# A block-sparse attention and gated feed-forward kernel: PSUM tiles of the last output blocks, a crossbar transpose for the second segment, and a new written-out order

## The chip, the core and the metric

The kernel runs on one core of a Trainium2 chip. A core has engines that run side by side, each taking its own instructions strictly in order: TensorE (PE, matrix products, with its weight loads shown apart as PEld), VectorE (DVE), ScalarE (ACT), GpSimd (POOL) and SyncE (SP), which issues DMAs. Products land in PSUM, and DVE or ACT copy them to SBUF. The metric is the device time of one execution in microseconds, the median of several runs. Lower is better.

## The reference

Inputs are q, k, v of shape 4 x 8 x 768 x 64 (batch, heads, tokens, head width), three sampled key blocks for each of the 24 blocks of 32 tokens, and the weights of a feed-forward part. The result has shape 4 x 768 x 512.

```python
scores = scale * np.matmul(q, k.transpose(0, 1, 3, 2))
# kept: neighbouring blocks, first and last block (as query or key), the sampled ones
scores = np.where(mask, scores, -1000000000.0)
attn = np.exp(scores - max); attn = attn / sum
x = np.matmul(attn, v)                  # then heads side by side: 4 x 768 x 512
h = np.maximum(x @ w_in, 0.0)           # 512 -> 1024
conv_out[s] = conv_w[0] * h[s-1] + conv_w[1] * h[s] + conv_w[2] * h[s+1]
gate = 1.0 / (1.0 + np.exp(-conv_out))
out = (h * gate) @ w_out                # 1024 -> 512
```

## The kernel before

**Segments and units.** The 4 x 768 query rows are cut into nine segments (`SEGS`): seven of 384 rows, numbered 0 to 6, then segment 7 with 256 rows and segment 8 with the last 128. The attention is cut into 144 units. A unit is eight score blocks of 128 x 128: up to eight score products into one of two PSUM tiles `st` (L761, 1024 columns in all), one exponential of 128x1024 on ACT (L773) into one of six tiles `pt`, and eight products with V, 65 columns each (L798; the 65th column is the row sum). The mask rides along as 24 extra rows of the score product. A segment of 384 rows has 18 units, four head pairs (hp) of 4.5 units each.

**After a head pair.** DVE takes the reciprocal of the sums (L707) and the normalised product (L709) into `xtok`. Then `xtok` is turned so that features lie on partitions (`xT`). Segments in `X_PE` do it on PE (L728, three products of 128 columns for a head pair of 384 rows, into a PSUM tile `mix`) and copy the result out with DVE or ACT; all others do it with one crossbar DMA that SP issues (L718).

**Feed-forward of a segment.** Eight first products (f1, L895) of four matmuls each go into one of two PSUM tiles `mix`; ReLU on ACT (L915) or DVE (L917) writes `hE`; the convolution is six multiplies (L947) and two adds (L955) on DVE for each pair of feature chunks (in segment 8 it is done on PE, L966); the sigmoid is a tanh on ACT (L994, L971), then L997 and L1002 on DVE write `gT`. A row block of 128 rows (t = 0 to 5 in a batch) is finished by the second products (f2, L830): four steps a = 0 to 3 of two matmuls with 512 columns each, step a needing the gates of chunk pair a. Then a copy to SBUF (L327 on ACT or L331 on DVE) and an output DMA on SP (L839).

**The last blocks.** `out_block` is called with `tail` for the two blocks that end with segment 8, t = 4 and t = 5 of the last batch. Before, they accumulate in halves of the two `st` tiles, which hold scores until then: block 4 in the left half of `st0`, block 5 in two pieces of 256 columns in the right half of `st0` and the left half of `st1`. Blocks 2 and 3 use the two `mix` tiles. Blocks 2, 3 and 4 need segment 7's gates; block 5 needs only segment 8's.

**The order.** No scheduler runs when the kernel is built. All operations are listed in a graph, and the string `ORDER` (found beforehand by a search over a model of the program; two characters name an operation, one its engine where it has a choice, one each buffer it takes) says in which order they are put down, and so in which order each engine runs them. `put_down` (L95) reads it. Costs and due times in the graph serve only that search.

**The start.** PE begins with `NWARM` + `NFILL` dummy products (L230): 13 of 256 and 26 of 128 columns, the latter strewn among the first real ones. Head pair 0 is loaded in fp32 over SP and ACT's queue, cast, turned on PE and copied to the slot tiles `t`; the mask rows are built on DVE meanwhile.

**Loads.** From head pair 6 on, q and k are also turned by crossbar DMAs of SP (L597, tiles `stg`), then copied by DVE (L331). SP runs them in the order of the string, together with L718 and the output DMAs.

Of the kernel before, what the change touches and what calls it, by code (L numbers as in the profile page):

```python
# [20 lines left out]
0G0002119030405060F18011a0708090a0b0c0d0e0H0f0g0h0i0I0J0M0N0R0O0Q0P0ZA1uV00S0T1wA0YA1xA1y01E11zV01FA0WV0VA0U0j
0k0l1B00m0n0o0p1N11O1I01Z01/21AA202b1171CV1DV11G1vA0XV520535715810V5401G012V1HV1b0q0r0s0t0u0v0w0x0y5c00z5911P1
0A5d0K1S02d32e1V12725h11MA0135e25i5501QV11UV1TV1RV565a5b1J05m05n5j32r04M2p2140B5f0C5v15w5o45g5k5x51LV1KV1+V10L
1e11f5A05B2102415C05F15G0D0E5K05L5l5p5H15M25q15y22V225V26V23V5T15U5V35r02cV25z5D5s155Y05Z5E2f15+4611625I5J2i0
6352gV3660676802hV2kV2jV5N5O5W06b16c5X1W15/6d16k06l60646p16m26q65695P15Q6r3161i1XV2qV36a6e6g26h1h6u06v6f16n6o
6z16A6s6t6w46i06I06J1YV1j1k1d5t16x6y6B56N16C6O5uV06jV6K06D6P15R16S06T6U26L06M6E26F5SV6G00+6HV6X16Q1o6Y2s4N2l34O
2D04P1p1m2F14Q1c1n2G4R1q4S2EV42R16Z31lih1ii70071ie0ifigV0ijA7917a724ik1il2807e07f7b5iC0iEiD29V2aViFimA7g06R7j1
7k7l1in16VioipV6W7o07p2t06+iG7x17y6/iw173ix7q27z34T1r4U2T24ViK1iL2uV47502vViM767C07DiyA7417c7d7H17E47I2w17h7i
2m02xV2oV2yV7m7M07n7r7s7A07B7J52nV7N7t1iN77178V12SV07F7R17Siq0iriH7O07T17uiIisViJ0iO7+07/7G7K7L831848028537v1
2H07P7wV2IV07Q8807UiP7W22JViQ7V1898d181827X8a42U4W1s8e86it1iuivV4X1t4Y2+2iR8f58m08n7Y0878b7ZV8r18s8o08c2K18g8t1  # L30
iS2iT2MV8w08x8hiz08y28B18C8i02LV8jiAiBViV8p0iU8G08H8q8u8v8k18D3i+3j0iWi/8I48O18P8Q5j608T08U8V0322iX8z8A8E8F8J
8Y18K18R8S8Z2W02V12X8lV2ZVj12YV8+1910j792932j2jc1jd9919a8W8X8/90j39e09f944Z3034+31iYiZ2/V1959b3j8je9g59j19kj4
8L1j50/331349628M8N2jfjgV09l136V39j9jaA19o09p9q4jl13a03c9t1jmji0jnA35V9u971gjjjkV9B03e04/370509Cjr1js9c09d9v0
2z0512N1jG0jHjI3b3i9G19H2A09hjJ2CV2BVjK9D29L09i9MjtA9I39m9N5jo1jpjqV9Q1jx09Rjy9n9r9sjLjzA9S19Y09wju1jvjwA9Z3l
3m13o38V29x19EjO1jMjPjQjR9y0jW29+4a119F9Ja2jX9zjA0a60a7a30a823j13n3u3x3y2jSjT9K9O9P2O12PVjN2QVjZjYab19Tac9U9/0
jBjCV9V1983fjU9Wag0j+jb3q13d33p4ad3jD1aha0ai5jEjFAao1apa4a59Ak23ks0a9k3jV9Xk4k5k6aq1j/aaaeafat0auajak1ay1arav4
kg1asazkhaA0aD0awktaEaxk7aL1aMaBaCk0k1aF2kiku3raN3aQ0aRk8k9aGkjaS1aHkvkkA2al2am3hV3AaV1aWa+0a/3v2kwA3aX5b00aI0
aJ3gV3sV3C0ky1kz3kV3kAV1kB0kCkDVkW0kXkZaO0b31aPb4b52kN1aTbb0kH0aU3z3G3H03J3K33M3L3R3S1kIkOkJAkPAbcbg1bhbd4kY3tV
k+kE0kFkGVl21l3l4l5l6aYaZb1b2b6bl0kK1b71bebmbi3bfbq1kLbrkMVb81an0km0knbjla2lck/bn1by0lb3wV43B0ldbzl0b9kokpbs5l7
bA0kqA1bD1kT1bEkUbI0bJkQ0bF2kVAbK4l8leaKkxkl3N1kRkSVli3lkl11lfbN1l9ljlgllbkbobpbtbubv2lmka1bObP3bS0bT3Dlhbw3EV  # L40
3FVbU1kbkckdbB0keA3b+1b/c05bCbGbHlw0bLc30c4lxc81lnbMbQc9lq1lrc50ba3Ololpbxcd0ce3U3V03Z3Wkf3XjhlybRlzbVbW1ca2cf4
3PV13QVlAV2c1cl1cmcq0c2lscrcn3lC0lDcv13IV03TV1bX0bYcwcs1ltcx5lEVlF0lGlBlHVl+0l/m0m1m2cA0cBc6c7cblI0cF1cccGluA3
cC046471lJcgchlL1co0cH2lMcN0cpctcOlKAlNVci1m61m7cjcucS1cTm3cylO0lR1cP3cU13+0bZ1cX0cYczlPcDcElScZ5lQAm8m9cIcJ1m4
mamb3Y43lTVme2mgmfcK2mccLmhm5d01d1d80cQcRcVcWc+d9lU0lVd24da0dd1lWVdec/lX1df24b4849ck4c13/di0djd3lYdn1domdmidk3
d4cMdb04k4l2lZAdcmA0ds0dtmu14424adgdp1mm3momnmpd50mqdhd6du4mjmkml4pdA1dBmBdld7dC0mr40V242msdF0dGdmdqmvdrdvdw1
dK1dLdDdEdH2mCmwdIdP0dQdM3dR1mtmDmEV0lvdX1dYdx1dymxdJdNdOdSe00dTdZ44m4h4dmyA24ykre1e51e20e6e75mS0mV1mWd+0mTdz2
41VdU2dVea0ebef1mUV0mXAne0nfngnhni4q0dW4z3d/ege34n4i04D4Am/1e4ec3mY0en0eon0n1V4oeh1e8es1ete9edmZ4eV3m+V4fVnm1nn
45V2ep4njnknpnoeeeiek0elnqnl0mF4E1mzex0eymG1mHmImJez0eu5n20eC0mKA3eDej1eqereK1n3eE3em4rn4AeLeM4nrevn51n6eP0eweA
n7VeQeBeFeGeN0nb0eU1eVnu2eH1eInweR5eW0n81ncn9naAeZ0e+f21eOf3e/3nvnxmM1mNeSeTeXeYfa0f44ndVnsny4jV3nznC3fbf0f1nt
f5ff1f61fgfc5fh0mOeJmPnDnEfdfk0o00flnFfefp1o1mQA1o31fqo4nGnH4sV4nAnB4tVo2Afm3nInJo5AnQ0nR4B4v4w14CmRmL4Ffx0fy  # L50
4xV4oq0osfr2nSnK1fz4fC1fDnTfH04J4K2fIfE14LV0orotounUV0fJ5ovnLnMnNfM1fNnOA2f724GV0f84HVfifR0fjnW0nXnZ1n+fnfO0nYA
n/AfS4ufofsftfZ1f+o90owoxfA0oaoi1okfT3ojfu0olfvomg20fBg3fFo61o7f/2g44obAg71fGfKfLg8fPfQo8Voy2fUozfW1onnVf904g4I
fwof0gc0g91oBoooAopgdge5oc1odoeAgk1ogohAglfV1g0g1g5gp0gm0oU1gqg6gaoVgu1gbgvgfggoO0oPoCoG3oHoJoIfXoKgr3oDgw2gn0
gD0gogsgtgEgI1gJoLgh2oEoFgigF4fYgK1oWgxoQgN0gOoMoNoXoYV1gP5gygW1oRgXp41p5p6g/0p7gjoSA3h0gY0gz0p8A0pa0pbpd1peh41
pcV1pfVpy0gAh13pAh5hd0pj0pg1pkphgG1h62nPoZplApiAhegHgLhi1gMgQgRhf4pzpBgB0gCA1gZ0g+hjpp1pG1pCpHpIpJpKhn0hk1pDpq
pm0pnpoAprAgS1gThohw1pO2pPpEpRhxhy5h2h3h7h8ps0pto+1o/hg1p0hhpuAp1h92pQpLhp0pMpF1pShahB1gU0hChlhmhqhrp2A2gVAhs0
hthD3pv1pwhb0hz0hK0pxAhcVpThLhM2pNhu0hvVhAhT1hUqh1hEqipW3pYqn0hY0hG1qoqjApXpZp+hV4hF1hNhOq21p/hZi51i6qpApUhHpV
q0hP2q3hW0hI0q4q1h+1q5hJV2hXqe0qfhQqy0qAqzi70qBh/i01i8i9q6A1qk1qgAi10i2i30qlqO1qq2ia1qrqPibi4AqmAp9p3qtqsqG3q80
q9hR1hSAqaic1idAqbqcA0rf1rgrhAr60r7quqvqCqIqRqwq7qdoTqxr8AqDrx0rc1rdryreAri1rjr90raqEqFrz2rk0r01rAqHrBqJrlrmqK
qQrs0rtr1rbArn1ru2qW0rorp0rqrrqLqXrC0rI1rO2rJrPrvqSrwqMqTqUqNrDrQrKrRrLrMA2rSArNqVr2rTr3r4V1r5qYqZq+A0q/rErF  # L60
# [53 lines left out]
def kernel(  # L114
# [701 lines left out]
    def out_block(b, t, due, deps, after, tail=False, last=False):  # L816
# [1 line left out]
        halves = ((0, 256), (256, 512)) if last else ((0, 512),)  # L818
        outs = []
        for x, (c0, c1) in enumerate(halves):  # L820
            mb = Buf(P_tail if tail else P_mix)
# [4 lines left out]
            prev = None
            for a in range(4):
                def fn(e, a=a, acc=acc, c0=c0, c1=c1):
                    for ffc in (2 * a, 2 * a + 1):
                        nc.tensor.matmul(out=acc(), lhsT=gT_t[gb.index][:, ffc, 128 * t:128 * t + 128],  # L830
                                         rhs=woutb[:, ffc, c0:c1], start=(ffc == 0), stop=(ffc == NFFC - 1),
                                         skip_group_check=True)
# [41 lines left out]
    relu = {}  # L874
    for n, (b, g, tok, C, _) in enumerate(SEGS):
        lastn = n == NSEG - 1
        base = T(ustart[n + 1]) + 4
# [6 lines left out]
        for fg in range(NFFC // FB):  # L884
# [18 lines left out]
            def rl(e, fg=fg, hb=hb, heb=heb, tok=tok, C=C, FB=FB, w1=w1):  # L903
# [12 lines left out]
                else:  # L916
                    nc.vector.tensor_scalar(out=dst, in0=src, scalar1=0.5, scalar2=0.0, op0=ALU.mult, op1=ALU.max)  # L917
# [18 lines left out]
        for pr in range(4) if b not in WHOLE else ():  # L936
# [51 lines left out]
            else:  # L988
# [13 lines left out]
                    nc.vector.tensor_tensor(out=gT_t[gtb.index][:, f0:f0 + 2, t0:t1],  # L1002
                                            in0=m_t[cb.index][:, 0, :, 0:w],
                                            in1=hE_t[heb.index][:, f0:f0 + 2, 1 + t0:1 + t1], op=ALU.mult),
# [45 lines left out]
```

## Time and profile before

| | us |
|---|---|
| median of 3 runs (207.68 to 209.1) | 207.83 |
| the profiled execution, its own time | 207.34 |
| span of that execution in the profile | 205.5 |
| outside the span | 1.8 |

Instructions in the span: 6234. The granted TensorE clock is 0.996 of full speed on the mean. In the profile, busy time of PE is the time in which a product is under way; products overlap, so the rate is read from rows that merge several products in a row. "PEld" rows are weight loads, one for each product. In the chain of waits every row is a start, a duration, the engine and the line. An `xcount` is the number of instructions merged into a row.

### The profile page before, as it was taken

The numbers are of one execution on the slowest core, as the hardware profiler recorded it, in microseconds if no ns is written. First come the engines' busy times: TensorE is split into PE (matmuls) and PEld (weight loads), VectorE is DVE, ScalarE is ACT, GpSimd is POOL, SyncE is SP. The second block draws the span as 40 slices with busy tenths as digits, with TensorE's granted clock in tenths as the row PEclk, the third lists the DMA queues.
The fourth block names the chain that finished last, engine by engine and source line by source line (L and its number), as shares of the span: only waits on it lengthen the run. The fifth ranks groups of instructions, "written<-read, shape, count | busy, mean of one in ns | idle before, by whom it ended". The sixth has DMA issues, their size and how long they took to land.

```text
span 205.5 us, 6234 instructions
## 1 busy us (share of the span) xinstructions
PE 198.0 (96%) x2395; PEld 142.9 (70%) x2415; DVE 185.2 (90%) x575; ACT 190.7 (93%) x252; POOL 60.8 (30%) x114
## 2 busy tenths in 40 slices
PE   7999999999999999999999999999999999999991
PEld 5678877877667766666677767677577757786750
DVE  5999999999999999999979977999999929999970
ACT  6999999999999999999899999999999988998842
POOL 8897555302733243202343248500000000000000
PEclk9999999999999999999999999999999999999998
DMA  6999999991889998994979399996521131011205
GB/s 138 206 193 188 186 148 148 153 180 27 107 107 150 153 182 131 134 170 66 196 96 121 71 120 175 172 200 116 148 82 26 23 126 46 3 51 56 102 9 198
DMA packets 49305, 25.20 MB, mean 123 GB/s; under 512 B 35100, under 2 KB 46332, under 8 KB 49276
## 3 DMA queue, kind: packets, MB, share of 16 engines
q0 software_dynamic: 19728, 11.05, 44.9%
q1 hardware_dynamic: 29260, 13.46, 30.9%
q8 instruction: 19, 0.31, 0.6%
q10 hardware_dynamic: 288, 0.30, 0.4%
q14 instruction: 10, 0.08, 0.1%
HBM read 23.09 MB, written 6.29 MB: 143 GB/s over the span
## 4 chain that ended last, share of the span: by engine, by line
PE 72%; ACT 18%; DVE 4%; issue 3%; DMA 2%; ACTq 0%
PE st L761 22%; PE mix L830 17%; PE mix L895 17%; ACT pt L773 15%; PE av L798 12%; DMA o2s<-in_k_dram 2%; DVE m L947 1%; PE st L830 1%; DVE t L331 1%; ACT t L327 1%; PE av L966 1%; ACT nat L327 1%; PE mix L728 1%; ACT o2s L327 1%; ACT m L994 0%
## 5 line engine op out<-in xcount | busy, mean ns | idle before, releaser
L773 ACT ACTIVATE pt<-st 128x1024 bf16<-128x1024 f32 x144 | 141.0, 1044 | 2.6 <-PE st L761 1.6
L761 PE MATMUL st<-t 88*128 88x256 bf16 (+2 forms) x600 | 91.7, 267 | 0.9 <-ACT t L327 0.2
L798 PEld LDWEIGHTS <-pt 128*128 128x128 bf16 x1152 | 53.7, 97 | 13.1 <-ACT pt L773 0.4
L761 PEld LDWEIGHTS <-t 88*128 88x128 bf16 x600 | 48.8, 97 | 19.9 <-issue 1.2
L798 PE MATMUL av<-vt,pt 128*128 128x65 bf16 x1152 | 60.0, 193 | 0.1
L895 PE MATMUL mix<-xT,winb 128*128 128x384 bf16 (+2 forms) x288 | 54.7, 307 | 0.3
L947 DVE TENSOR_SCALAR m<-hE,cw 128x382 bf16<-128x382 bf16 (+2 forms) x192 | 48.5, 313 | 0.3
L830 PE MATMUL mix<-woutb,gT 128*128 128x512 bf16 x157 | 44.4, 379 | 0.6
L955 DVE TENSOR_TENSOR m<-m 128x764 bf16<-128x764 bf16 (+2 forms) x64 | 34.1, 534 | 0.6
L895 PEld LDWEIGHTS <-winb 128*128 128x128 bf16 x288 | 24.1, 97 | 9.0 <-issue 1.0
L994 ACT ACTIVATE m<-m 128x764 bf16<-128x764 bf16 (+2 forms) x32 | 26.7, 835 | 0.6 <-DVE m L955 0.6
L830 PEld LDWEIGHTS <-gT 128*128 128x128 bf16 x200 | 17.3, 97 | 10.2 <-DVE gT L1002 0.6
L407 POOL COPY pace<-pt 1x1 bf16<-1x1 bf16 x24 | 7.7, 322 | 53.4 <-ACT pt L773 53.4
L917 DVE TENSOR_SCALAR hE<-mix 128x384 bf16<-128x384 f32 x26 | 14.5, 556 | 5.7 <-PE mix L895 5.3
L915 ACT ACTIVATE hE<-mix 128x384 bf16<-128x384 f32 (+2 forms) x38 | 18.4, 501 | 0.9 <-PE mix L895 0.5
L1002 DVE TENSOR_TENSOR gT<-m,hE 128x764 bf16<-128x764 bf16 (+3 forms) x36 | 18.2, 511 | 0.6
L709 DVE TENSOR_TENSOR xtok<-av,rcp 128x384 bf16<-128x384 f32 (+2 forms) x36 | 18.3, 507 | 0.5
L239 POOL DMA_DIRECT2D nat<-in_q_dram x23 | 17.1, 743 | 2.3 <-issue 1.0
L331 DVE COPY t<-mix 64x384 bf16<-64x384 bf16 (+1 forms) x33 | 13.3, 411 | 0.8 <-PE mix L460 0.3
L997 DVE TENSOR_SCALAR m<-m 128x764 bf16<-128x764 bf16 (+3 forms) x36 | 12.1, 337 | 0.5 <-ACT m L994 0.3
L239 POOL DMA_DIRECT2D nat<-in_k_dram x15 | 11.4, 762 | 2.7 <-issue 2.1
L331 DVE COPY t<-stg 64x1536 bf16<-64x1536 bf16 x20 | 11.5, 578 | 0.3
(73 smaller groups left out, 119.9 us busy)
## 6 DMA issues: line engine op xcount, KB each, us to landing
out_dram<-o2s SPq DMA_DIRECT2D x23, 256.0 KB
nat<-in_k_dram POOLq DMA_DIRECT2D x15, 192.0 KB, 4.7
vn<-in_v_dram POOLq DMA_DIRECT2D x15, 192.0 KB, 5.7
...
```

The costliest lines, as they stand in the source:

```text
L239: return op(name, {eng: occ}, lambda e: on(e).dma_start(out=dst(), in_=src), prio, deps, dma=(kind, service), **kw)
L331: nc.vector.tensor_copy(out=dst, in_=src)
L709: nm = op("norm", {"DVE": t_dps(128 * C)}, lambda e: nc.vector.tensor_tensor(out=xtok_t[xk.index][:, 0:C].rearrange("p c h d -> p h c d"), ...
L761: nc.tensor.matmul(out=st[:, 128 * x:128 * (x + n_)], lhsT=t[0:88, 12 + 6 * hh + kc, :], rhs=t[0:88, idx:idx + (n_ - 1) * (2 if P < NPE el ...
L773: nc.scalar.activation(out=pt_t[ptb.index][:, c0:c1], in_=st_t[stb.index][:, c0:c1], func=AF.Exp, bias=0.0, scale=0.125)
L798: nc.tensor.matmul(out=o[:, off:off + 65], lhsT=pt_t[ptb.index][:, 128 * x:128 * x + 128], rhs=V_t[vslot_b[P].index][:, hh, kc, 0:65], sta ...
L830: nc.tensor.matmul(out=acc(), lhsT=gT_t[gb.index][:, ffc, 128 * t:128 * t + 128], rhs=woutb[:, ffc, c0:c1], start=(ffc == 0), stop=(ffc == ...
L895: nc.tensor.matmul(out=mix_t[hb.index][:, w1 * y:w1 * y + w1], lhsT=winb[:, fc, 128 * ffc:128 * ffc + 128], rhs=xT_t[xt_buf[n].index][:, f ...
L915: nc.scalar.activation(out=dst, in_=src, func=AF.Relu, bias=0.0, scale=0.5)
L947: nc.vector.tensor_scalar(out=m_t[cb.index][:, x, y, 0:w], in0=hE_t[heb.index][:, f0 + y, t0 + x:t0 + x + w], scalar1=cw[:, x, f0 + y:f0 + ...
L955: nc.vector.tensor_tensor(out=m[:, a_, :, 0:w], in0=m[:, a_, :, 0:w], in1=m[:, b_, :, 0:w], op=ALU.add)
L994: th = [op("tanh", {"ACT": t_act(2 * w) + 0.04}, lambda e, cb=cb, w=w: nc.scalar.activation(out=m_t[cb.index][:, 0, :, 0:w], in_=m_t[cb.in ...
```

## The change

```diff
-    P_tail = Pool_("tail", 2 * NST)
+    P_tail, P_fx = Pool_("tail", NST), Pool_("fx", 20)
...
-    NWARM, NFILL = 13, 26
+    NWARM, NFILL = 13, 32
...
-    X_PE = (0, 1, 7, 8)
+    X_PE = (0, 7, 8)
...
-            mb = Buf(P_tail if tail else P_mix)
+            mb = Buf(P_tail if last else P_mix)
 
             def acc(mb=mb, c0=c0, c1=c1):
-                t_ = st_t[mb.index // 2][:, 512 * (mb.index % 2):512 * (mb.index % 2) + 512] if tail else mix_t[mb.index]
+                t_ = st_t[mb.index] if last else mix_t[mb.index]
                 return t_[:, 0:c1 - c0]
...
-                          [ld_wout[a]] + deps[a] + (last_exps if tail and a == 0 else []),
+                          [ld_wout[a]] + deps[a] + (last_exps if last and a == 0 else []),
...
+            fx = []
+            for f in range(FB * fg, FB * fg + FB):
+                if f % 2 == 0 and tok + w1 < S:
+                    near[(n, f // 2)] = Buf(P_fx)
+                    fx.append(near[(n, f // 2)])
...
-                   [f_prev, he_zero[0], he_zero[1]], alloc=[heb] if new else [],
-                   uses=[hb] + ([] if new else [heb]))
+                   [f_prev, he_zero[0], he_zero[1]], alloc=([heb] if new else []) + fx,
+                   uses=[hb] + ([] if new else [heb]) + (
+                       [near[(n - 1, f // 2)] for f in range(FB * fg, FB * fg + FB) if f % 2 == 0] if g else []))
...
-                    due + 3.7, [g1], uses=[cb, heb] + ([] if newg else [gtb]), alloc=[gtb] if newg else [])
+                    due + 3.7, [g1], uses=[cb, heb] + ([] if newg else [gtb]) + ([near[(n, pr)]] if (n, pr) in near else []),
+                    alloc=[gtb] if newg else [])
```

- **Last blocks.** Only block 5 of the last batch now takes `st`: its two pieces have a whole `st` tile each. Block 4 accumulates in a `mix` tile, like blocks 2 and 3.
- **Second segment.** Segment 1 leaves `X_PE`: its four `xtok` tiles are turned by four crossbar DMAs on SP (L718) in place of twelve PE products (L728) and four copies.
- **Links.** A buffer that stands for no memory (`near`, pool `fx`) ties a segment's ReLU to the gate product beside it and to the next segment's ReLU. Its number is read from the string and used nowhere else.
- **Dummies.** 32 in place of 26 products of 128 columns.
- **Order.** The whole string is new. Compared engine by engine, the two programs differ in few kinds of work: PE loses the twelve transposes and gains six dummies; seven copies of segment turns remain on DVE in place of eleven; ACT makes 16 output copies in place of 19 and DVE 9 in place of 6; SP issues 24 crossbar turns of `xtok` in place of 20. The rest is moved by a few microseconds at most, and the next part names the places.

More of the change, by code (lines that the diff above doesn't have):

```diff
@@ L20 @@
 ORDER = """
[L21 to L60, printed above, removed]
@@ L61 @@
-rGA3rH
+0M0N0S00010211j0T0W1T01U1O0030405060708090a0b0c0d0e0f0g0h0i0j0k0l0m0n0o1i0U0V1e1g1d0L0O0P0Q13A12V1AA11CA1E01K1
+0p0q1DA0Y1h0Z1H00+1FV01f23025217G0r0s0t0u0/A10A1GV0R16V1IV1LA580595d111A1BA18V1JV5e0v0w0x0y0z0A1M00B0C0D0E0F0G
+262h12j31/1191NV1V15a05f10X1SA05i05j0H0I1Y05n15k22k2v25o1WV11XV5b05c5g5h1ZV1+V1b24V15p35s05t5l5m1k11l5B15C5u4
+5D50J5q5r1a5G05H2702a15I05L15M5v28V22bV0K5w15E5Q05R5N12cV29V1P11QV1RV5S25Z15+5F5J5K620635x02iV25O5/32l064467168
+2o15P5y6956c06d5T5U6006e02mV32qV2pV2nV6h16i5z1616q06r65666j12wV31s5AV05V15W6s26v16w6a6b6f6g6x36A06B6k2d22x14S2y
@@ new lines @@
+6l15X06C46F16G6H56t6u2016y1c1p1o6m26n21V22V6O06P6Q06z6D6E5YV1t6I6T16U6J6o11u4T2r34U2J04V2L01v4W2M4X1w4Y6R06Y06S
+6Z6K02X16L6V16M06pV7116W726NV4Z1x4+ig1ih6+276077733784ij0ik1q1niiV001r7e17filViE06X2e12fViF7g52gV7j02Z24/2+507k
+im0in6/iHiG7l0ioV17o17p7q1iI70ip17t07u747v275iq7B17C792z07D3irViM17G07H7a12AV42BV7I4iJiy17L1iz7h2C07M7i7N52KV4
+iAV27Q07m2s17n7R7r7S02DV2EV2uV2tV7b1is07siN7V17W7cit7w810827X11y511z5234253363543755147d17x7E07F832iPiuV3iO861
+877y2iQ883iR7z7J7K7Oiv18b0iw8c8g18hiKixViU27P2N07T8d42Q17UiL02OV02SV3007A382318i58o08p7Y7Z18485898a8e8t18u7+0
@@ new lines @@
+3912/1iViW7/iX2PViS8q02RA8f8y08z8v1iB18j8k8r08s8D18E8A28F3iC8w8I08J8x8B8C8K48l1iT8miDVj03j1iY8Q18Rj332Vj22YV0
+j808V08W8S58X0iZ33Vi+j4i/1535V1j9je18+18/930jf8G948H8n80901952j5j68L8M18N28T8U8Y9b18Z913a929c9g09d39h96jg97jaj7
+9i53f9819l19mjh8O999n4jb9q09r9v1jcA0jiV19s1jn1jo3cV3bVjk01m3g13d03i9wjl562F0jpA9x03eV23h3o9D09Ejt1ju9F29I19J9e0
+9fjmV9j3r3s09k9o2G0jI0jJjKjL2HVjM2IV9N09OjvA9K3jq1jr9P5jsV57jQ1jR3k09p9t9S1jz09T9u9+0jN9/jOjSjPjw19yjx9A0jT9BjU
+9U42T13u3p13t3j38P23w1a01jyAjA9z1jBAa31a4a809Ga99H2U1jF09L9M9Q9R9Ca50aa2jV2VV2WVjGad1jC1aeai0aj9a3v43laf39V9WjD
@@ new lines @@
+jY2j+3AjZa10a2a6a7abacaq1aragjWjHAj/jXjEVk43k59X2k0ak5as4ku09Yav0awax1k1k6k7k8kv3D3B23E23G3F3M3N0ahki1aA1aBkj
+aF0aGk2k3aC0alam1atauayazaDaEaN1aOk9an0aH2kwkkaS0aTaP33P3Q3aIkakbkxaokyV2aX1aYkl3qV3aJ9ZaU5b00b1kA0kBkmV3aZ4b51
+b6kD1b20b71kCV143x3mV3zV3nVaQ0bd0kEkFAkJ0kKkLAbeaRbi1aVbjkG1bf2aWkM0kNbk3bn0kHbobs1a+bta/kOA5kIA6kY0k+kZaK1kP0
+3Sb3b4kV1k/aL3yVbp5bu4bA0bBl413CV4l5l03R3X3Y1l6b8kQb91l7kRVlc2ldlebgkWbC0kXAl1bhbF1bGblbK0bLkS1kTbH1kUA7bM2ba2
+l8bbbmbqko0brbvkpl9bwbP1bQbD0lflk3bR3kzjjap0bU0kc1bVbW5kqjdkr3I03T1aMlglll2l31kdbEbIbJc01bNbObS3Jc1c50c6lhksA2
@@ new lines @@
+c24bTkely0c70bx0lalmlbln3H03Ubcbylilolzca1cb3+lpkfbXbY1cf0c3c4c8cgcc1kgA13KVljlqlrc9lAlBbz3LVch2lCA0ls1cn1cocs0
+ctlE0lFkh3VV13WV3OV0bZ1b+lGVcp3ltcx1cylH0lIcu53/1434041lJVm00m1m2m3m4cz4cC0cdcDlu3ZV1cH1cIcecilvcE0cJ1lwA1m5cP0
+lK0cjcQcq0crcU1lN1lLck2clcR3cVlOcvcwcAcBcZ0c+4ccFcGcK4d0lPAcW5m6m7lMVm81m9mambc/4lQ1lRd21d3lT0da0cM0mclSAcL1db
+lUd40lW1lXdf14hdc1mdcS440cTcNlVVdgdh3mg2mhmib/1cmlYVmjmedk0cXcYdllZ0l+4ed0d1d5d6d71mf42494a2dm2l/Alxmkmo3mpmqmr
+d8msdp1dqdd0mw1dr5dedu0dvdw0mlmC045didjdC1dndodsdDdE1mxdtmDdxdy1dH0dIdM1dNmtmmmndJ3mudz2mvdFdGlDd9cOdO54q4f4r2
@@ new lines @@
+4v4i1mEmydR0dSdKmzdT2dZ1d+d/0mF4bV2e20e3dLdPdQdUdVmAV1dAdW1e71e8e00mU1e41mVmWV08mGA0dB24s4gec0ede146V247VdXe95
+ee2ktmX0mYmZAng0nidY4n4o0m+14jeh1ei4w04Eep0eqn10n248ej4e5knm/e6eaebeu1evefer0egekel1es4F34J4tnhn3Vnjn0A9ew1ez0
+eAeB5n70no1npnqeE1n8eFetexn414GeM0eNey4uem0nknren4pV3nsn9AeG2eO0eCn5n6VaeR1eSna0eDeHeInbeT1ntncAbeoeW0eXmI1mJ
+e/1nd0eP0eQmKf0neeUeVmLnw2eJ2eKny4kV34lVnxnznleY5f12nAnfVnE3nunmnFnGmMA2eLf40f5f60nn0nHfc1fdeZfe1nBnImO0e+mPfh0
+f2fio51fm1f3mQo6mR4Hfj5fnfr0f7o7AnJmSA3f81fffs4x4yV4fgfo2ft0nS14zVnvnCnKo20o3nDnTf91o4VnLos1fz1oufAfB1otovow4B
@@ new lines @@
+4C14I4PnU4AmNmB4K14L4DA4fkfE0fFnM0nNfG3fJ1fKnVnOnPnWV2fa4MV04Q24NVfO0flfpfqfufPfL4nQA1fvoxfQ54RV0n/1nY0o0nZo1A
+n+AfT1fUfC0fDfHf/0g0ob1ocfV2oyozfw0fxg10g41g5o80o9odAg90fIgafMoe1ofok0olomonoog61oaVopoA2oBoqoCorfNfRge1gfgb3
+oh0oDgg4oifSgm0gnfWfX1g2g3g7g8gr1ojAfb0fynXnR4OogAfY2oW04moEgo5oFgcgdoQ1gsgw0gxghoXgigt2fZmHoI3oJoKoLoGoRoMgy0
+gj1oHgkgp0gqgugvgF1gGgzgK0gAoSoNoOoPgH1f+mTgLoYgP1gM3oZoTgQgY0gZgI1gJoUA2gB0gCo+V1g+4gR5glp60p7p8p9h10h2pc1pd
+paV0pf0pgh32peV1cphVpA1pBpCh61h7h80gNpi1pjpDpl0pmpkAdpnAgOhf0gShghk1gTpo1hlpI0oVpJhh1hm3pKgU2pEpr0pspphp0pqAehq
@@ new lines @@
+hy1g/0h0h4h5h9ptAgD1hr5gEA1pLgVgW0pMpNpFhahi1hjhnhohsgXVhb1pQ2pRpSpThcpu0hzpGpvp01pwAfp1hthD0hEhu0hA4hd0hF2pU
+heVpOhvpH1pPp2p3px0pyp4A3hM1hB0hw1pzAhxVhNhV0hCpY3pZhGhI2p+p/q0hWqp0hH1pVhO0qj1qkpWhJpXhX1qqh+1hPp5h/hQhR1i70
+qlAgq1qrAhq2q3i03q41i8q5hY0hK0q6q7hZhLA2i95q8A2qg0qhqA0qBhSqDqQ1qCqiAii1i21iaqm1ibi30i4i50i6AqnqoAjqa0qbqEqs2qt
+qFhT1qcic2quidhUAie1qdifArh1riqeA3r80r9rjAqvqGqwqI3qKrz0rAqJqHqLre1qxraAqyrB0qRrfpbo/qzrb0rcrgAqTqMrk1rlrdAq9qf
+ru0rm2r21rvrp1rqrnrCror3rDqSqNrr2rsrtrQ0rK1rw0qUrxqOryrE0rLrFrRqPqVrMrSrNr4qWqXr5r6A0rOV1rGrTrUArHrPr7rIV2rVrJ
@@ L62 @@
+qY1qZq+q/r0A3r1
 """
@@ L872, in whole_gate @@
         return [got[2 * a:2 * a + 2] for a in range(4)]
-    relu = {}
+    relu, near = {}, {}
     for n, (b, g, tok, C, _) in enumerate(SEGS):
```

## The prediction

> **What bounds the kernel now.** I read the page's sums and the shares of the chain of waits first, then that chain in order of time (start, us, engine and line), then the timeline of single engines where the change works.
>
> ```profile
> PE 198.0 (96%) x2395; PEld 142.9 (70%) x2415; DVE 185.2 (90%) x575; ACT 190.7 (93%) x252; POOL 60.8 (30%) x114
> PE 72%; ACT 18%; DVE 4%; issue 3%; DMA 2%; ACTq 0%
> ```
>
> ```profile
> 30.06 1.63 DVE m L947 x6
> ...
> 57.22 0.48 PE mix L895 x2
> ...
> 101.51 0.65 PE mix L895 x4
> ...
> 121.04 0.44 PE st L761 x4
> ...
> 122.79 0.48 PE av L798 x16
> ...
> 147.08 0.43 PE mix L830 x2
> ```
>
> Three engines are nearly full, so busy shares do not decide; the chain does. It runs on ACT until about 30 us, for a few us on DVE (from the row at 30.06), and from about 38 us almost wholly on PE. The merged rows give PE's rate: a unit's scores 0.44, sixteen V products 0.48, four f1 matmuls 0.65, two f2 matmuls 0.43. The kernel has 144 units (63.4), 1152 V products (34.6), 64 f1 chunks of four matmuls (56 of them, and 8 more for segments 7 and 8 together, by 0.65: 41.6) and 24 blocks of eight f2 matmuls (41.3): 181 us that no order of work can shorten, in the 194 us from the first exponential to the last product (7.3 and 201.3, by the rows of start and tail below). The other 13 hold transposes, the convolution of segment 8, fixed costs and the few waits. So an edit that helps DVE, ACT or SP is worth nothing by itself; work taken off PE counts, and so does a new wait of PE.
>
> **The twelve transposes of segment 1.** They go from PE; four copies go from DVE, four crossbar DMAs come to SP.
>
> ```profile
> L728 PE MATMUL mix<-ident,xtok 128*128 128x128 bf16 x36 | 4.6, 219 | 0.0
> L331 DVE COPY xT<-mix 128x384 bf16<-128x384 bf16 x8 | 2.7, 350 | 0.2 <-PE mix L728 0.2
> ```
>
> ```profile
> 8.87 0.50 PE L460 MATMUL mix<-ident,nat 128*128 128x128 bf16 x6
> ```
>
> A transpose is recorded with 219 ns, but six in a row took 0.50 us, so one delays the next by (0.50 - 0.22)/5 = 0.056 us. I take 12 x 0.056 = 0.67 us off PE. The bounds: 0, if they stood in gaps of PE, and 12 x 0.219 = 2.63, if each had run alone; the row of six is the nearer, since PE has other products queued at 38 to 48 us. The four copies free 4 x 0.35 = 1.4 us of DVE, which buys nothing where PE is the bound.
>
> The Trainium skill ("TensorE: Matmul & The Clock Gate", Part 4: PE-mode transpose) gives about 275 ns for such a transpose in a kernel and says that transposes do not count as activity for the clock; by 275 ns the edit would be worth 3.3 us. The row of six contradicts that price here; it comes back as a rival.
>
> **The crossbar in their place.** First the durations of SP's turns, then SP's timeline, then DVE's around them.
>
> ```profile
> L718 SPq DMA_TRANSPOSE xT<-xtok x20: 1178/1212/2267, 56.6 to 163.1; - x20
> ```
>
> ```profile
> 41.82 3.88 SPq L597 DMA_TRANSPOSE stg<-nat  x3
> ...
> 96.93 1.18 SPq L718 DMA_TRANSPOSE xT<-xtok  x1
> ```
>
> ```profile
> 46.63 0.54 DVE L709 TENSOR_TENSOR xtok<-av,rcp 128x384 bf16<-128x384 f32 x1
> ...
> 57.19 1.12 DVE L331 COPY t<-stg 64x1536 bf16<-64x1536 bf16 x2
> ```
>
> SP is held 1.21 us by each. The crossbar issued at 96.93 was the last that the f1 matmuls around 101.51 waited for, so issue to use is at most 4.6 us. In the new list SP runs the turn of head pair 3 of segment 1, then that of head pair 2, then the second half of the turn of attention pair 7, which before was the last of the three issued at 41.82. So that half now waits behind an instruction that needs the normalised product of 46.63 to 47.17. Let this product come up to 2.5 us later (next part): 49.7; the two turns are issued by 52.1, the later one is usable by 50.9 + 4.6 = 55.5, and f1 of segment 1 wants it at 57.2. Pair 7's half is issued at 52.1, usable by 56.7, and DVE's copies of it stand at 57.19. Both are covered by the scores, V products and f2 steps that PE runs in between, the second by only 0.5 us. I take 0; without that cover the cost would be the lateness itself, since DVE runs in order.
>
> **The new list between 27 and 39 us.** Before the first normalised product of segment 1, DVE now has three ReLUs more (ACT did these before), four copies of turned q more, and one multiply of two instructions less.
>
> ```profile
> L917 DVE TENSOR_SCALAR hE<-mix 128x384 bf16<-128x384 f32 x26 | 14.5, 556 | 5.7 <-PE mix L895 5.3
> ...
> L331 DVE COPY t<-mix 64x384 bf16<-64x384 bf16 x23 | 8.0, 350 | 0.3
> ```
>
> ```profile
> 35.83 0.54 DVE L947 TENSOR_SCALAR m<-hE,cw 128x382 bf16<-128x382 bf16 x2
> 36.40 0.56 DVE L709 TENSOR_TENSOR xtok<-av,rcp 128x384 bf16<-128x384 f32 x1
> ```
>
> That is 3 x 0.556 + 4 x 0.350 - 0.54 = 2.5 us: the product ended at 36.96 and now ends near 39.5. Behind it waits PE's first V product of head pair 2 of segment 1, which takes the same PSUM tile. But PE's list also puts more ahead of that V product, counted from the first f1: six f1 chunks in place of five (0.65) and 11 units of scores in place of 8.5 (2.5 x 0.44 = 1.1). So 1.75 of the 2.5 is covered. The open 0.75 is the upper bound; the lower is -0.5, since ACT has three ReLUs less in the stage in which it ends the chain. I take +0.2, as PE's own transposes and their waits leave the same stretch.
>
> **Start and dummies.** ACT's timeline up to the first exponential, and a run of dummies on PE:
>
> ```profile
> 6.02 0.40 ACT L327 COPY t<-mtok 24x256 bf16<-24x256 bf16 x1
> 6.45 0.48 ACT L327 COPY t<-mix 64x384 bf16<-64x384 bf16 x1
> 6.95 0.35 ACT L327 CAST nat<-o2s 128x192 bf16<-128x192 f32 x1
> ```
>
> ```profile
> 7.75 0.68 PE L230 MATMUL av<-warm 128*128 128x128 bf16 x9
> ```
>
> ACT ends at 7.30 there and the first exponential follows. By the new list ACT gains a second cast like that at 6.95 (0.35) and two short mask copies (about 0.4 each by the row at 6.02), and loses a key copy like that at 6.45 (0.48) and a longer mask copy (0.40 at least): +0.3 at most. I take 0, from -0.3 to +0.3. Six dummies at under 0.68/9 = 0.08 us are at most 0.5 us; they stand where PE waits for the first casts and copies, which hide them; if not, 0.5 is lost.
>
> **The tail.**
>
> ```profile
> 198.09 0.29 DVE L997 TENSOR_SCALAR m<-m 128x512 bf16<-128x512 bf16 x1 [0.28 <-ACT m L994]
> 198.29 0.76 DVE L1002 TENSOR_TENSOR gT<-m,hE 128x512 bf16<-128x512 bf16 x2
> ```
>
> ```profile
> 199.11 1.94 PEld L830 LDWEIGHTS <-gT 128*128 128x128 bf16 x10 [0.22 <-DVE gT L1002]
> ...
> 201.57 0.59 ACT L327 COPY o2s<-st 128x512 f32<-128x512 f32 x1 [0.23 <-PE mix L830]
> ```
>
> DVE's last gate product ends at 199.05; PE, which had run out of work 0.22 us before, then has ten full matmuls left, and ACT copies the last block. By the new list block 2, whose first half ran earlier before, stands whole at the very end; after the last gate product come 2 matmuls of block 3, 2 of block 4, 2 of half width of block 5, 2 of block 4 and all 8 of block 2: 15 full ones by columns. Five more at 0.43/2 are +1.08 us, and block 2 has to wait for the copy that clears block 3's `mix` tile (0.59 plus 0.23 to notice, against 1.08 of PE work meanwhile): +0.1.
>
> On the other side, DVE's run from segment 6's first ReLU to that last product loses the normalised product of segment 7's first head pair, now placed in an idle stretch ahead, and the 0.28 wait, behind which two other gate instructions now stand:
>
> ```profile
> L709 DVE TENSOR_TENSOR xtok<-av,rcp 128x256 bf16<-128x256 f32 x4 | 1.7, 421 | 0.1
> ```
>
> So -0.42 - 0.28. The separate tiles themselves remove no wait that the profile shows. Tail: 1.08 + 0.1 - 0.70 = +0.5, from 0 to +1.2.
>
> **The sum** is -0.67 + 0 + 0.2 + 0 + 0.5 = 0.0. Made against the profiled execution (207.34, of which 205.5 is its span) it gives 207.3; the median of the runs is 0.5 higher, so 207.8 on that scale. The two added links alter no instruction: their numbers are read and dropped, and whatever they do is in the list.
>
> **The rivals.**
> 1. *DVE becomes the bound from 27 to 39 us.* For it: the chain itself is on DVE at 30.06 and all of segment 0's ReLUs now are in its queue, each freeing a PSUM tile that PE's next instruction takes. Against it: PE's list was moved back by 1.75 us. If PE waits for the whole 2.5 instead of the 0.2: 207.8 + 2.3 = 210.1, slower. It decides as soon as PE reaches those instructions 2 us before DVE.
> 2. *The crossbar is late.* If turns do not overlap and each takes 4.6 us, pair 7 is usable at 49.7 + 3 x 4.6 = 63.5, 6.3 after DVE's copy: 214.1. The point is 57.2. Against it: three were issued within 3.88 us.
> 3. *Each transpose cost PE its 219 ns*, with its wait for DVE: 2.63 in place of 0.67 gives 205.8, and 205.3 with the tail at 0, faster. Against it: the row of six. This is what the page named above would have (205.2 by its figure).
> 4. *The transposes filled gaps, and the tail costs its full 1.2:* 207.8 + 0.67 + 0.7 = 209.2.
>
> **How the numbers follow.** Changes under 1% (2.1 us) are about what a measurement of this kernel can tell from none. Chances: forecast 0.57, rival 1 0.16, rival 2 0.04, rival 3 0.08, rival 4 0.15. The forecast's own bounds (list 0.2 from -0.5 to 0.75, tail 0.5 from 0 to 1.2, start 0.3 either way) run from 207.8 - 0.7 - 0.5 - 0.3 = 206.3 to 207.8 + 0.55 + 0.7 + 0.3 = 209.4; stretched to rival 1, the range is 206.2 to 210.2, which leaves out rival 2 and most of rival 3. Slower by over 1% (above 209.9): rival 2 and most of rival 1, 0.18. Faster (below 205.75): most of rival 3, 0.07. The rest, 0.75, is within 1%.
>
> **What would show it.** In the new profile PE should still carry most of the chain from 40 us on. f1 of segment 1 should start without a wait for a DMA. DVE's first normalised product of segment 1 should come near 39.5. After DVE's last gate product PE should show sixteen weight loads of f2 (two of them for half widths) where ten stood, and the time from segment 6's first ReLU to the final copy should be about 0.5 us longer. It would be wrong if PE showed a wait for DVE near 30 to 39 us, or if `st` tiles had held the tail back in a way that no row shows.

## The result and the profile after

The changed kernel takes 209.47 us (median of 15 runs, 208.77 to 211.19) against 208.14 of the kernel before in the same series (207.43 to 211.56): a ratio of 1.0065, 95% interval 1.0035 to 1.0094. So it is slower by 0.7 to 2.0 us, less than the 1% called "no change" in the prediction, but its whole interval lies above 1. The profiled execution was the slowest of the 15 (211.19, span 209.2), so its largest stall has to be compared with a second profile before it is believed.

The page of the changed kernel, busy times and the shares of the chain of waits:

```profile
PE 198.9 (95%) x2391; PEld 143.4 (69%) x2409; DVE 185.0 (88%) x571; ACT 190.8 (91%) x252; POOL 61.3 (29%) x114
...
PE 53%; ACT 20%; DVE 18%; issue 4%; DMA 3%; SPq 0%; POOL 0%; ACTq 0%; DVEq 0%
```

PE is as busy as before, but the chain left it: 53% in place of 72%, DVE 18% in place of 4%. More of DVE in the chain, with DVE's busy time unchanged, says that the chain runs back through something that PE had to wait for. The list of PE's waits holds one large entry, a crossbar turn; its row in PE's timeline (start, us; in brackets the idle time ahead and who ended it):

```profile
124.15 0.49 PE L895 MATMUL mix<-xT,winb 128*128 128x384 bf16 x2
126.75 0.48 PE L895 MATMUL mix<-xT,winb 128*128 128x384 bf16 x2 [2.12 <-DMA xT<-xtok]
```

These are f1 products of segment 4. Followed back in the chain of waits:

```profile
111.16 0.55 DVE xtok L709
...
117.71 0.47 DVE xtok L709
...
118.93 0.46 SPq L718
...
119.43 7.28 DMA xT<-xtok
```

SP's timeline in the same stretch, first of the changed kernel, then of the kernel before:

```profile
112.73 1.23 SPq L597 DMA_TRANSPOSE stg<-nat  x1
114.01 0.56 SPq L839 DMA_DIRECT2D out_dram<-o2s  x1
118.20 2.49 SPq L718 DMA_TRANSPOSE xT<-xtok  x2
120.79 1.24 SPq L597 DMA_TRANSPOSE stg<-nat  x1
```

```profile
110.14 3.41 SPq L597 DMA_TRANSPOSE stg<-nat  x2
114.07 5.70 SPq L718 DMA_TRANSPOSE xT<-xtok  x2
```

The product of head pair 2 was ready at 111.71, that of head pair 3 at 118.18. Before, SP issued pair 2's turn at 114.07 and then waited for pair 3's product. In the new order the turn of pair 3 stands ahead of that of pair 2. SP runs in order, so it sat idle from 114.57 to 118.20, and the turn that could have gone out at 114.6 went out at 119.43, behind the other. Its 7.28 us to landing fall together with five loads that POOL issues between 116.46 and 120.29.

In this execution the wait had a sequel. Windows of 1 us (length, then busy us of PE with its instructions, of PEld, DVE, ACT and POOL; then the granted clock, the DMA share, which passes 1 where transfers overlap, and GB/s):

```profile
125.00:126.00 1.00, 0.00 (x0) 0.00 (x0) 0.00 (x0) 0.71 (x1) 0.15 (x1) 1.00 1.27 211
...
128.00:129.00 1.00, 1.00 (x5) 0.47 (x4) 0.96 (x3) 0.90 (x2) 1.00 (x2) 0.50 1.31 297
...
132.00:133.00 1.00, 1.00 (x21) 0.79 (x18) 0.99 (x3) 0.88 (x2) 0.72 (x1) 1.00 1.29 190
```

About 1 us after the wait the granted clock fell to 0.50 for some 3.4 us (from about 127.9 to 131.3, by the mean clocks of these windows), which by estimate costs another 1.7, half of that time. So 3.8 of this execution's surplus of 3.9 over the profile before (211.19 - 207.34) sit here. The median's surplus is a third of that; what the usual execution loses, and whether the start (first exponential at 7.82 in place of 7.32) and the end play a part, the experiments have to tell. The ratios below leave out runs that the chip disturbed, the medians do not; of seg1_xbar that leaves two runs, of loads_later five.

### The profile page after: what moved, and what is told of

It is laid out like the page before. It is cut to its first block, busy times and chain, and to the rows that moved or that the text cites. A ratio compares the mean times of both kernels' runs of the same rounds, so it can differ in the third digit from the quotient of the medians.

```text
span 209.2 us, 6221 instructions
## 1 busy us (share of the span) xinstructions
PE 198.9 (95%) x2391; PEld 143.4 (69%) x2409; DVE 185.0 (88%) x571; ACT 190.8 (91%) x252; POOL 61.3 (29%) x114
## 4 chain that ended last, share of the span: by engine, by line
PE 53%; ACT 20%; DVE 18%; issue 4%; DMA 3%; SPq 0%; POOL 0%; ACTq 0%; DVEq 0%
ACT pt L773 18%; PE st L761 16%; PE mix L830 14%; PE mix L895 13%; PE av L798 8%; DVE m L953 5%; DMA xT<-xtok 3%; DVE t L331 3%; DVE m L961 2%; DVE hE L917 2%; DVE gT L1008 1%; DVE m L1003 1%; PE st L830 1%; DVE mtok L299 1%; DVE xtok L709 1%
## 5 line engine op out<-in xcount | busy, mean ns | idle before, releaser
L761 PEld LDWEIGHTS <-t 88*128 88x128 bf16 x600 | 49.3, 98 | 22.8 <-issue 2.8
L895 PE MATMUL mix<-xT,winb 128*128 128x384 bf16 (+2 forms) x288 | 55.5, 311 | 2.3 <-DMA xT<-xtok 2.1
L830 PE MATMUL mix<-woutb,gT 128*128 128x512 bf16 x166 | 46.5, 379 | 0.6 <-DVE rcp L707 0.2
L895 PEld LDWEIGHTS <-winb 128*128 128x128 bf16 x288 | 24.6, 98 | 11.9 <-issue 3.7
L327 ACT COPY o2s<-mix 128x512 f32<-128x512 f32 x15 | 9.0, 603 | 4.1 <-PE mix L830 4.1
```

Of the source, the lines that this page charges most:

```text
L761: nc.tensor.matmul(out=st[:, 128 * x:128 * (x + n_)], lhsT=t[0:88, 12 + 6 * hh + kc, :], rhs=t[0:88, idx:idx + (n_ - 1) * (2 if P < NPE el ...
L895: nc.tensor.matmul(out=mix_t[hb.index][:, w1 * y:w1 * y + w1], lhsT=winb[:, fc, 128 * ffc:128 * ffc + 128], rhs=xT_t[xt_buf[n].index][:, f ...
```

## The experiments

Kernels of one series ran on the same chip beside the kernel before. Times in us:

| run | median | lowest | before, same series | ratio to before, 95% interval |
|---|---|---|---|---|
| again | 209.11 | 208.59 | 207.97 | 1.0044, 1.0008 to 1.0079 |
| turns4 | 208.21 | 207.69 | 207.97 | 1.0006, 0.9975 to 1.0038 |
| tail_old | 209.40 | 208.78 | 207.97 | 1.0049, 1.0017 to 1.0082 |
| front_old | 209.49 | 208.45 | 207.97 | 1.0073, 1.0034 to 1.0112 |
| swap_before | 208.31 | 207.44 | 207.87 | 1.0008, 0.9980 to 1.0035 |
| seg1_xbar | 212.86 | 208.96 | 207.87 | 1.0127, 1.0057 to 1.0197 |
| turns_all | 207.99 | 207.76 | 207.87 | 1.0016, 1.0002 to 1.0030 |
| loads_later | 210.23 | 208.88 | 207.87 | 1.0103, 1.0059 to 1.0147 |
| seg1_late | 208.20 | 207.34 | 207.79 | 1.0010, 0.9985 to 1.0035 |
| front_turns | 208.64 | 207.82 | 207.79 | 1.0040, 1.0023 to 1.0057 |
| tail_turns | 208.26 | 207.82 | 207.79 | 1.0016, 0.9991 to 1.0042 |
| three_old | 207.66 | 207.41 | 207.79 | 0.9998, 0.9987 to 1.0010 |

### The changed kernel again

No edit.

> The changed kernel itself, once more, as the measure for the other three and for a second profile. The profiled execution of the change (211.19 us) was 1.7 us above the median of its runs, and the wait of PE for segment 4's crossbar (3.6 us with the slower clock behind it) lies in it. Theory A, the wait is part of every run: the second profile shows f1 of segment 4 waiting again for xT at about 124 us, 2 us and more, and the time is again near 209.5. Theory B, the wait was an accident of that one execution: no such wait in the second profile, and the time is still near 209.5, so that start (+1.0) and tail (+0.9) have to carry the slowdown.

The profiled execution took 208.84. The turn is late again, 5.92 us after its issue in the chain of waits, and PE waits for it:

```profile
119.63 5.92 DMA xT<-xtok
```

```profile
124.36 0.49 PE L895 MATMUL mix<-xT,winb 128*128 128x384 bf16 x2
125.59 0.49 PE L895 MATMUL mix<-xT,winb 128*128 128x384 bf16 x2 [0.75 <-DMA xT<-xtok]
```

The wait belongs to the kernel, but here it is 0.75 us and the clock stays at 1.00. The 2.12 us and the half clock were seen in one execution only.

### Segment 4's two turns in their old order

Two entries of the order's string change places, `cO` (turn of head pair 2) and `d9` (head pair 3):

```diff
-mvdFdGlDd9cOdO54
+mvdFdGlDcOd9dO54
```

> One pair of instructions on SP changes places: the crossbar turn of head pair 2 of segment 4 is issued ahead of that of head pair 3, as before the change; nothing else. Theory A (the late turn costs PE in every run): 1 to 3 us less than the changed kernel, and f1 of segment 4 starts without a wait for xT. Theory B (an accident of one execution): the same time within 0.3 us.

0.9 us less than the changed kernel, in the median and in the lowest run alike, and by the ratio no different from the kernel before. SP's timeline and then PE's, of this run:

```profile
114.94 4.42 SPq L718 DMA_TRANSPOSE xT<-xtok  x2
```

```profile
124.12 0.81 PE L895 MATMUL mix<-xT,winb 128*128 128x384 bf16 x4
```

Pair 2's turn goes out at 114.94, the wait is gone and four f1 products run through. Theory A holds, just below its 1 to 3 us: one pair of instructions on an engine that only issues transfers carries most of the slowdown.

### The end put back

```diff
-    P_tail, P_fx = Pool_("tail", NST), Pool_("fx", 20)
+    P_tail, P_fx = Pool_("tail", 2 * NST), Pool_("fx", 20)
...
-            mb = Buf(P_tail if last else P_mix)
+            mb = Buf(P_tail if tail else P_mix)
...
-                t_ = st_t[mb.index] if last else mix_t[mb.index]
+                t_ = st_t[mb.index // 2][:, 512 * (mb.index % 2):512 * (mb.index % 2) + 512] if tail else mix_t[mb.index]
...
-                          [ld_wout[a]] + deps[a] + (last_exps if last and a == 0 else []),
+                          [ld_wout[a]] + deps[a] + (last_exps if tail and a == 0 else []),
```

and the order of before from the first f1 product of segment 8's last head pair on.

> The end alone goes back: the tiles of the last blocks are halves of the st tiles again, block 4 among them, and from the first f1 chunk of segment 8's last head pair on the order is that of before. If the end costs what the two profiles show between that chunk and the final copy, 0.9 us less than the changed kernel; by the sum of the prediction 0.5 less; if the new end is worth something and the loss is elsewhere, 0 or more.

No gain: 0.3 us more than the changed kernel, inside both intervals. The 0.9 of the first reading was a mistake: it compared the copy of block 2 in both kernels, but before, block 4's copy came last. Measured from the same f1 product to the last copy's start, the ends are equal. PE's timeline of the kernel before, and then of the changed one:

```profile
190.98 1.19 PE L895 MATMUL mix<-xT,winb 128*128 128x128 bf16 x13
```

```profile
194.94 1.25 PE L895 MATMUL mix<-xT,winb 128*128 128x128 bf16 x14
```

The changed kernel's DVE, PEld and ACT rows at its end (one fence for each engine's timeline):

```profile
201.47 0.43 DVE L1008 TENSOR_TENSOR gT<-m,hE 128x512 bf16<-128x512 bf16 x1
```

```profile
201.95 3.04 PEld L830 LDWEIGHTS <-gT 128*128 128x128 bf16 x16 [0.20 <-DVE gT L1008]
```

```profile
205.57 0.59 ACT L327 COPY o2s<-mix 128x512 f32<-128x512 f32 x1 [1.83 <-PE mix L830]
```

Before, 201.57 - 190.98 = 10.59; after, 205.57 - 194.94 = 10.63. Inside, the parts moved against each other as the prediction said: sixteen weight loads after the last gate product where ten stood. But DVE's last gate product ends 6.96 after that f1 product in place of 8.07 (199.05 - 190.98).

### The start put back

```diff
-    NWARM, NFILL = 13, 32
+    NWARM, NFILL = 13, 26
```

and the order of before up to the seventh exponential.

> The start alone goes back: 26 dummies in place of 32, and up to the seventh exponential the order is that of before. If the first exponential's delay of 0.5 to 1.0 us is carried to the end, 0.5 to 1.0 us less than the changed kernel; if PE's list takes it up by 36 us (ACT ends the chain up to about 30 us, PE after it), 0.

No gain either. ACT's timeline, the first exponential of the changed kernel's second profile, then of this run:

```profile
7.82 1.94 ACT L773 ACTIVATE pt<-st 128x1024 bf16<-128x1024 f32 x2
```

```profile
7.18 1.94 ACT L773 ACTIVATE pt<-st 128x1024 bf16<-128x1024 f32 x2
```

The first exponential is 0.64 us earlier, yet f1 of segment 4 begins no earlier, and the wait is still there. PE's timeline of this run:

```profile
124.50 0.49 PE L895 MATMUL mix<-xT,winb 128*128 128x384 bf16 x2
126.20 0.48 PE L895 MATMUL mix<-xT,winb 128*128 128x384 bf16 x2 [1.21 <-DMA xT<-xtok]
```

124.50 against 124.36 in the second profile of the changed kernel. The first ReLU of segment 0 still leads (28.84 against 29.18), that of segment 2 no longer (80.31 against 80.16); what takes the lead up between was not followed.

### The inversion alone, in the kernel before

`cM` (pair 2's turn) moves behind `d7` (pair 3's):

```diff
-3d4cMdb04
+3d4db04
...
-dBmBdld7dC0
+dBmBdld7cMdC0
```

> The kernel before with one thing changed: the crossbar turn of head pair 2 of segment 4 is issued behind that of head pair 3, as the changed kernel has it. Theory A (the order of these two turns is what the change costs): 0.6 to 1.2 us slower than before (208.6 to 209.2), with a wait of PE for xT ahead of f1 of segment 4. Rival (the swap costs only together with the new list around it): within 0.3 us of before.

In the chain of waits of this run the turn lands 5.11 us after its issue, and PE's row of six f1 products is 1.38 long where the kernel before has 1.14:

```profile
120.13 5.11 DMA xT<-xtok
```

```profile
124.40 1.38 PE L895 MATMUL mix<-xT,winb 128*128 128x384 bf16 x6
```

```profile
124.11 1.14 PE L895 MATMUL mix<-xT,winb 128*128 128x384 bf16 x6
```

So the inversion costs PE 0.24 us here; the ratio of 1.0008 says 0.17, with an interval from -0.4 to 0.7. That is what the rival expected, within 0.3 us of before: alone the inversion costs little, and only together with the new list around it 0.9. The five profiles that show this turn late form a series: it landed 5.11, 5.92, 5.95 (the run with the old end), 6.36 (the run with the old start) and 7.28 us after its issue, and PE waited 0.24, 0.75, 0.80, 1.21 and 2.12. What decides beside the late issue is how long the turn is under way: in the second profile of the changed kernel it went out 4.73 us ahead of the first f1 product (119.63 and 124.36), here only 4.27 (120.13 and 124.40), and yet it was later there.

### POOL's loads out of the way

Three of POOL's loads (`4s`, `4g`, `4o`), with a copy between them (`4n`) and two attention turns of SP (`4j`, `4w`), go behind `4E`, the copy on POOL that waits for a later exponential:

```diff
-dB24s4gec0
+dB2ec0
...
-dY4n4o0m+14jeh1ei4w04Eep0
+dYm+1eh1ei4E4s4g4n4o04j4w0ep0
```

> The changed kernel with its inverted turns, but three of POOL's loads that were issued at 118 to 120 us (two of q, one of v) wait for a later exponential and come at about 124 us, after the time in which the late turn is under way. If the turn is late because it shares the DMA engines with these loads, it lands about 1 us or more sooner after its issue (5.9 to 7.3 us before), PE's wait for xT goes, and the time is 0.5 to 0.9 us less than the changed kernel; if the late issue alone does it, the wait and the time stay.

Half of it came true. Windows of the changed kernel and of this run, DMA share the last number but one:

```profile
120.00:123.00 3.00, 2.97 (x24) 1.82 (x24) 2.05 (x6) 3.00 (x4) 0.28 (x1) 1.00 2.19 148
```

```profile
120.00:123.00 3.00, 2.95 (x30) 1.92 (x30) 1.88 (x6) 3.00 (x4) 0.00 (x0) 1.00 1.31 139
```

In the second profile of the changed kernel the share is 1.80. With three loads fewer beside it the turn, still issued second and late, is in time: PE's timeline of this run has four f1 products in a row.

```profile
124.78 0.81 PE L895 MATMUL mix<-xT,winb 128*128 128x384 bf16 x4
```

The turn goes out at about 120.1 and the third product, which needs it, starts at 125.11, so it took at most 5.0 us in place of 5.92. That f1 starts 0.42 us later than in the second profile covers only part of its wait of 0.75. So the loads beside the turn look like the second ingredient, but that rests on one profile. The share of this window alone does not order the runs: the kernel before has 1.95 and no wait, its last turn having gone out about 1 us earlier; the run with the old start has 1.35, and its turn took 6.36. The Trainium skill says ("DMA: Bandwidth & Descriptors", Issuing engines are not separate DMA queues): DMAs that sync and gpsimd start run on the same 16 DMA engines and interleave. This trace is in line with it: a wait of 0.75 with the loads beside the turn, none without.

But by the ratios the kernel lost some 1.2 us against the changed one, and its trace shows that the moved transfers were themselves needed. DVE's timeline, then PE's:

```profile
139.03 1.14 DVE L331 COPY t<-stg 64x1536 bf16<-64x1536 bf16 x2 [2.77 <-DMA stg<-nat]
```

```profile
140.22 0.81 PE L761 MATMUL st<-t 88*128 88x384 bf16 x6 [1.18 <-DVE t L331]
142.46 0.59 PE L830 MATMUL mix<-woutb,gT 128*128 128x512 bf16 x2 [1.30 <-DVE hE L917]
```

DVE waits 2.77 us for an attention turn (`stg`) that came late, and PE for DVE: 2.5 us in two places (a wait of 0.34 at the second stands in the changed kernel's second profile too). A load that is moved out of one transfer's way needs a deadline of its own.

### The turns of segments 1 and 2 too

```diff
-8n80
+808n
...
-9R9Ca50aa2jV2VV2WVjGad1jC1aeai0aj9a3v
+9R9a9Ca50aa2jV2VV2WVjGad1jC1aeai0aj3v
```

> The changed kernel with the turns of segments 1, 2 and 4 all issued in the order of the head pairs; in segment 1 that of pair 2 goes ahead of that of pair 3, in segment 2 that of pair 1 ahead of that of pair 2. If an inverted order costs only where f1 follows close behind (no wait is seen for segments 1 and 2), the same time as with segment 4's pair alone put right (208.2); if the other two cost too, 0.3 to 1 us less.

By the ratio 0.16% above before (interval 0.02 to 0.30%); with segment 4's pair alone it was 0.06%. The two inversions in segments 1 and 2 cost nothing that shows, and in both profiles of the changed kernel segment 4's is the only turn of `xtok` that PE waits for.

### Segment 1's transposes, alone

```diff
-    X_PE = (0, 1, 7, 8)
+    X_PE = (0, 7, 8)
```

in the kernel before, the four turns at the places of the four copies.

> The kernel before with one thing changed: segment 1 is turned by four crossbar DMAs at the places where its copies stood; twelve transposes of PE and four copies of DVE go. By the sum of the prediction -0.67 us (207.3); by the price of 219 ns each -2.6 us (205.4); if the transposes filled gaps of PE, or another engine ends the stretch, 0.

Slower than every expectation (the profile is of the fastest of its runs, 208.96). SP's timeline:

```profile
37.03 7.79 SPq L718 DMA_TRANSPOSE xT<-xtok  x3
44.99 0.81 SPq L239 DMA_DIRECT2D t<-mback  x1
45.90 1.22 SPq L597 DMA_TRANSPOSE stg<-nat  x1
```

Three turns that wait for their products one by one hold SP until 44.8. The attention turn that now goes out at 45.90 went out at 39.49 before, by this row of its SP timeline:

```profile
39.49 1.33 SPq L597 DMA_TRANSPOSE stg<-nat  x1
```

It and the three behind it go out 6 to 8 us later. DVE waits for them and PE for DVE:

```profile
51.71 0.56 DVE L331 COPY t<-stg 64x1536 bf16<-64x1536 bf16 x1 [1.08 <-DMA stg<-nat]
```

```profile
53.60 0.61 PE L761 MATMUL st<-t 88*128 88x384 bf16 x4 [0.98 <-DVE t L331]
```

So this run measured SP's queue, not the transposes. It was made again with three of the turns behind the attention turns.

> Once more the kernel before with segment 1 turned by the crossbar, but now three of its four turns are issued behind the three attention turns of 41.82 to 45.70, so that they hold nothing up on SP. The earlier form had lost nothing and won 0.07 us by 49 us and then stood behind those turns. Theory (ACT's exponentials pace 41 to 49 us, so that PE's twelve transposes stood in gaps): no wait of DVE for the attention turns, and the time of before within 0.2 us. Rival (PE is the bound there and the credit of 0.67 was right): 0.6 to 0.7 us less than before.

Against the kernel before, where f1 of segment 4 starts at 124.11, PE's timeline of this run:

```profile
124.10 1.14 PE L895 MATMUL mix<-xT,winb 128*128 128x384 bf16 x6
```

Twelve transposes fewer, same order otherwise, and at 124 us a gain of 0.01 us; the ratio is 1.0010 (0.9985 to 1.0035), which leaves out a gain of 0.67 (0.3%), and the lowest run is that of before (207.34 and 207.35). The theory holds. Its reason stands in the kernel before, in the chain of waits that the prediction read:

```profile
40.91 1.02 ACT pt L773
...
47.98 1.09 ACT pt L773
...
49.12 0.60 PE st L761 x4
```

From 40.91 to 49.07 the chain stays on ACT: eight exponentials and a tanh. ACT's own timeline has no idle time from 36.5 to 51.6, and all four groups of transposes lie in that stretch (at 37.91, 40.56, 44.05 and 48.08). What PE saved there it spent waiting for ACT.

This run's profiled execution (208.81) shows once more what a late turn costs: SP's timeline, then PE's.

```profile
136.32 3.36 SPq L597 DMA_TRANSPOSE stg<-nat  x1
139.79 1.27 SPq L718 DMA_TRANSPOSE xT<-xtok  x1
```

```profile
144.37 0.65 PE L895 MATMUL mix<-xT,winb 128*128 128x384 bf16 x3 [0.73 <-DMA xT<-xtok]
```

One turn took 3.36 us on SP, so the next one, issued at 137.57 in the profile of the kernel before, went out at 139.79. Why it took so long, the trace does not show.

### Start and end again, with the turns put right

The edits are those above, combined.

> The changed kernel with segment 4's two turns put right and the start of before (26 dummies, the old order up to the seventh exponential). If the start is worth nothing because ACT takes it up by about 30 us: the time of the kernel with the turns alone put right (208.2). If the start's 1.0 us was hidden in the first trial behind a longer wait for the crossbar (1.2 in place of 0.8 us): 0.4 to 1.0 us less than that.

> The changed kernel with segment 4's two turns put right and the end of before. From the first f1 chunk of segment 8's last head pair to the last copy's end both ends took the same time within 0.05 us in the profiles, so 208.2 again; by the prediction's sum for the end 0.5 us less (207.7).

> All three put back: turns of segment 4, start and end; what stays of the change is segment 1's crossbar and the list between. If the parts add up as measured one by one (turns 0.9, start 0, end 0), 208.2; if start and end cost what the first reading of the profile gave them, 207.0 or less, better than both kernels.

With the turns put right, the old start alone brings nothing (208.64, lowest 207.82, against 208.21 and 207.69), and the old end alone brings nothing (208.26, lowest 207.82). All three together are the kernel before in time (0.9998, interval 0.9987 to 1.0010). That is less than the sum that was expected (turns 0.9, start 0, end 0: 208.2). In the same series the run with both is 0.6 and 1.0 us below those with only one of them, and 0.4 in the lowest runs (207.41 against 207.82 twice). The run with the turns alone, made in another series, stands between: its lowest is 0.39 above that of before, with all three put back 0.06. So start and end together look worth about 0.4 us that neither brings alone; why, no run shows. No version beat the kernel before.

A second wait of the new list is left when the turns are put right. PE's list of waits from 120 to 165 us in turns4 (us in total, times, longest) has one entry:

```profile
PE mix L830 <- DVE hE L917: 0.4, 1, 0.4
```

Near 140 us an f2 step waits 0.34 to 0.38 us for a ReLU of DVE, in the second profile of the changed kernel and in all five profiles with the turns put right; the kernel before has no such wait. No run takes it away, and three_old has it and is not slower than before, so what it is worth stays open. Why front_turns has a median 0.4 above the kernel with the turns alone, with seven of its twelve runs near 209 and five near 207.9, was not followed up; what was late in those runs, no trace shows.

## Why the prediction was wrong

The range (206.2 to 210.2) held the time, but the forecast of no change missed a slowdown that is real, 1.1 to 1.3 us in the medians.

- **The step that failed: "The crossbar in their place ... I take 0".** The mechanism priced there, a turn behind an instruction of SP that waits for its product, was looked for only where the change says that it adds turns, in segment 1, and there the answer was right: f1 of segment 1 started without a wait for a DMA. But the whole string is new, and it inverted two turns of segment 4 that the change does not speak of; the sum has no term for them. Put right, they give back 0.9 of the 1.1 us; the rest is gone only in the run that has the old start and the old end together. The price of the step was too low as well: it allowed "at most 4.6 us" from issue to use, read from one turn. By that price the turn of 119.43 would have been usable at 124.0, ahead of f1 at 124.15, and the cost 0; in the four profiles of the inverted new order it took 5.92 to 7.28. Rival 2 had a late turn, at another place, with the same 4.6 and a chance of 0.04. The search would have needed one pass over SP's queue in the new order, asking of every turn whether the product it waits for is later than that of the turn behind it.
- **The credit of 0.67 us for the transposes** was wrong in size: it measured 0.01 at f1 of segment 4. The spacing of 0.056 us may hold; but the sum counted it as if PE ended the stretch "from about 38 us almost wholly", and the chain is on ACT from 40.91 to 49.07. Rival 4 had this half right; that its 209.2 is near the measured time is luck, since its other half, a tail of 1.2, did not come.
- **The tail**, +0.5 forecast, measured 0.04 from the first f1 product of segment 8's last head pair, and on the prediction's own measure, from segment 6's first ReLU to the end of the final copy, 0.3 us less than before (33.24 before, 32.94 and 32.95 in two profiles of the changed kernel). PE's part was right (sixteen weight loads; from the last gate product to the end of the last copy 4.26 us in place of 3.11, where the sum said 1.18 more); DVE's run up to it is 1.11 shorter from that f1 product and 1.44 from that ReLU, where the sum had 0.70.
- **The start**, 0 within 0.3, brought nothing when it alone was put back, though not by its own working: the first exponential came 0.5 us later, outside the bounds, and the delay is gone by 80 us.
- **The list from 27 to 39 us.** The first normalised product was forecast to end near 39.5. DVE's timeline of the changed kernel:

```profile
38.85 0.54 DVE L709 TENSOR_TENSOR xtok<-av,rcp 128x384 bf16<-128x384 f32 x1
```

It ends at 39.39, and PE shows no wait for DVE there, so rival 1 fell. Rival 3 fell with the transposes. Start, list and transposes together came to 0.04 and 0.25 us at f1 of segment 4 (124.15 and 124.36 against 124.11). That the two wrong terms, -0.67 and +0.5, nearly cancelled is luck: with the measured ones the sum would have been near 0 as well, and near 0.9 with segment 4's turns.
